# A planned attention and feed-forward kernel: new planner costs, first batch's inputs ahead of the weights, and a sign mask made by GpSimd

## The chip, the cores and the metric

The kernel runs on one core of one Trainium2 chip. Its time is device microseconds from start to end of one execution; the times shown are medians of several runs. The engines are TensorE (PE, matmuls; PEld is its weight load), VectorE (DVE), ScalarE (ACT), GpSimd (POOL) and SyncE (SP, which issues the DMAs here). Each works through its own instructions in the order in which they were written, and waits on semaphores for the others.

## The reference

```
def _attn_ref(q, k, v, p):                       # 8 batches, 8 heads, 576 tokens, head size 64, 32 packed
    def sm_attn(qq, kk, vv):
        s = scale * np.matmul(qq, kk.transpose(0, 1, 3, 2))
        a = np.exp(s - np.max(s, axis=-1, keepdims=True))
        return np.matmul(a / (np.sum(a, axis=-1, keepdims=True) + 1e-09), vv)
    p_packed = sm_attn(p, k, v)
    return sm_attn(q, p_packed, p_packed)

def _moe_ref(x, w_in, w_out, a, b):              # x 4608 x 512, w_in 512 x 2048, w_out 2048 x 512
    h = x @ w_in
    P = a[0] + a[1] * h + a[2] * h**2 + a[3] * h**3
    Q = 1.0 + np.abs(b[0]) * np.abs(h) + np.abs(b[1]) * h**2
    return (P / (Q + 1e-6)) @ w_out
```

The heads of the attention's output, side by side, are x. Both weight matrices arrive as float64, as pairs of 32-bit words.

## The kernel before, in words

The work runs over 8 batches. For each, `attention(bb)` transposes keys and queries, makes packed values `PPT` from the 32 packed queries, and leaves the transposed softmax weights of the second attention in `AH` (and a low part `AL` from batch 1 on). `m_chunk` multiplies PPT by a chunk of `win`, so that a hidden value takes only the 32 packed rows of each head. A *unit* is one batch, one half of the tokens (288) and one of 8 chunks of 256 hidden columns: 128 units in all. `hidden(bb, x, c)` makes the unit's hidden values h on PE, the polynomials P and Q on ACT, DVE and POOL, and the quotient by Ln and Exp on ACT. `acc_block` multiplies the result (`gh`, and its low part `gl`) by the output weights three units later (`LAG = 3`). The first 12 units (`PLAIN`) use float32 matmuls and later ones split operands into two parts (`split`: high part by ACT, low part `gl` by POOL).

The weights are loaded and converted in 16 *words*, each a block of 128 partitions x 1024 float64 (1 MB, in two DMAs): 8 chunks of `w_in` and 8 of `w_out`, sorted by the unit that first uses them (the first five are `w_in`). `load_words(n)` issues loads until n words are ahead of the converted ones. `convert()` (line 429) turns one word into float32 with two ACT instructions, one mask, and two more DVE instructions (a shift with OR, an integer add); all of them take every second 32-bit element of a row. The mask keeps the sign bit of the rescaled high half and is written where the low half was, so it follows the second ACT instruction, and the two other DVE instructions follow it.

`load(bb, what)` issues the DMAs of one input of a batch: keys `k0`, `k1`, values `v0`, `v1`, queries `q0`, `q1` (for batch 0 of 512 KB each) and the small pieces `r`, `p`, `qr`, `rv` for the remaining 64 tokens and the packed queries. `p` comes with a copy on POOL. The loop at line 923 lists, for batch 0, loads by name and, as numbers, how many words are to be loaded by then. `nc.pin()` behind it fixes the order of all this at the front of the queues.

Nothing else is issued in program order. `nc` is a `Planner`: it records all instructions, prices each one (`cost`, `price`, `transfer`), finds the dependences (`edges`) and simulates the five engines (`schedule`), alternately forward in time and backward to get ranks; it keeps the best of `ROUNDS` forward plans by its own reckoning, and `issue` then writes each engine's instructions in the order of their planned starts. A plan's error thus shows as an engine that waits in front of an instruction with ready ones behind it. `WAY` and `PASS` are delays from one engine's result to another's start, `DMA_ISSUE`, `DMA_DELAY` and `DMA_RATE` price a DMA. `idle` (line 992) puts small dummy matmuls with zeros into planned PE gaps of over 180 ns in the first 150 us of the plan, once the first `acc` matmul is out.

Of the kernel before, what the change touches and what calls it, by code (L numbers as in the profile page):

```python
# [13 lines left out]
F32 = mybir.dt.float32  # L14
F32R = mybir.dt.float32r
I32 = mybir.dt.int32
# [3 lines left out]
ALU = mybir.AluOpType  # L20
AX = mybir.AxisListType
PSUM = bass.MemoryType.PSUM

P = 128
# [7 lines left out]
class Planner:  # L32
# [4 lines left out]

    ENGINES = ("tensor", "vector", "scalar", "gpsimd", "sync")

    COST = {"vector": (70, 1.04), "scalar": (93, 0.83), "gpsimd": (215, 2.11), "tensor": (15, 0.417)}  # L40
    TRANSPOSE, F32 = (15, 0.834), (30, 1.667)
    WAY = {("vector", "vector"): 127, ("scalar", "scalar"): 143, ("tensor", "tensor"): 0, ("gpsimd", "gpsimd"): 0}
    WAY.update({(f"sync", x): 0 for x in ENGINES})
    PASS = 200
    ROUNDS = 4
    DMA_ISSUE, DMA_DELAY = 600, 2300

    DMA_RATE = 100.0, 190.0, 370.0

# [26 lines left out]
    def cost(self, engine, name, args, kwargs):  # L76
        if engine == "sync":
            return self.DMA_ISSUE
        fixed, per = self.COST[engine]
        if engine == "tensor":  # L80
            if name == "transpose" or args[1].dtype == F32:
                fixed, per = self.TRANSPOSE if name == "transpose" else self.F32
        aps = [x for x in args if isinstance(x, bass.AP)]
        if engine == "scalar":
            fixed += (aps[-1].space == PSUM) * -42 + ("accum_out" in kwargs) * 186 + ("bias" in kwargs) * 93
        if engine == "vector" and len(aps) > 2 and any(self.columns(x) == 1 for x in aps[1:]):
            fixed += 60
        if engine == "vector" and name == "tensor_scalar":
            per /= 2
        return fixed + per * self.columns(aps[1] if name.startswith("reduce") else aps[0])  # L90
# [13 lines left out]
    def price(self, engine, calls):  # L104
        if engine != "tensor":
            return sum(self.cost(engine, *x) for x in calls)

        parts = {}
        for name, args, kwargs in calls:
            part = args[1].offset // args[1].ap[0][0], args[0].offset // args[0].ap[0][0]  # L110
            parts[part] = parts.get(part, 0) + self.cost(engine, name, args, kwargs)
        return max(parts.values()) + 7 * (len(calls) - 1)

    def edges(self):

# [30 lines left out]
            edges.append(before)  # L146
        return edges

    def schedule(self, before, after, rank, back=None):

        n = len(rank)
        need = [len(x) for x in before]
        at, start, end = [0.0] * n, [0.0] * n, [0.0] * n
        soon = {e: [] for e in self.ENGINES}
        ready = {e: [] for e in self.ENGINES}
        free = dict.fromkeys(self.ENGINES, 0.0)
        for i in range(n):
            if not need[i]:
                heapq.heappush(soon[self.ops[i][0]], (0.0, rank[i], i))
        now = dma = 0.0  # L160
        left = n
        while left:
            for e in self.ENGINES:
                while soon[e] and soon[e][0][0] <= now:
                    heapq.heappush(ready[e], heapq.heappop(soon[e])[1:])
                if free[e] > now or not ready[e]:
                    continue
                _, i = heapq.heappop(ready[e])
                left -= 1
                start[i] = now  # L170
                end[i] = free[e] = now + self.costs[i]
                if e == "sync":
                    dma = max(dma, end[i]) + self.transfers[i]
                    end[i] = dma + self.DMA_DELAY
                for j in after[i]:
                    need[j] -= 1
                    f = self.ops[j][0]
                    way = self.WAY.get((e, f) if back is None else (f, e), self.PASS)
                    at[j] = max(at[j], end[i] + way)
                    if not need[j]:  # L180
                        heapq.heappush(soon[f], (at[j], rank[j], j))
            now = min(
                t
                for e in self.ENGINES
                for t in ([free[e]] if ready[e] else [max(soon[e][0][0], free[e])] if soon[e] else [1e12])
            )
        return start, end

    def order(self):
        n = len(self.ops)  # L190
        self.costs = [self.price(*x) for x in self.ops]
        self.transfers = [self.transfer(calls[0][1]) if engine == "sync" else 0 for engine, calls in self.ops]
        before = self.edges()
        after = [[] for _ in range(n)]
        for i, x in enumerate(before):
            for j in x:
                after[j].append(i)
        rank = list(range(n))
        best = None
        for r in range(self.ROUNDS):  # L200
            start, end = self.schedule(before, after, rank)
            if best is None or max(end) < best[0]:
                best = self.best = max(end), start, end
            s, e = self.schedule(after, before, [-x for x in end], True)
            m = max(end)
            rank = [m - x for x in e]
            rank[: self.pinned] = range(-self.pinned, 0)
        self.end, self.start = best[0], best[1]
        self.deps, self.t0 = dict(enumerate(before)), best[1]
        return sorted(range(n), key=lambda i: (best[1][i], i))  # L210
# [47 lines left out]
def attention_rational_ffn(  # L258
# [42 lines left out]
    nc = Planner(tc.nc)  # L301
# [76 lines left out]
    def load_words(n):  # L378
        while len(words_in) < min(len(words), converted + n):
            r = len(words_in)  # L380
            kind, i, n2 = words[r]
            used = [x for x, _ in words_in]
            free = [x for x, end in room if r < end and x not in used[converted:]]
            free = [x for x in free if x[0] is not w_ring or x[1] not in (2, 3) or started]
            if not free:
                return
            x = min(free, key=lambda x: max((j for j in range(r) if used[j] == x), default=-1))
            raw = x[0].at(x[1], [P, n2 * 512], I64)
            if kind == "in":
                c = i // 2  # L390
                for y in range(2):
                    src = w_in[2 * y * P : (2 * y + 2) * P, c * CF : (c + 1) * CF].rearrange("(x p) f -> p x f", p=P)
                    nc.sync.dma_start(raw[:, 512 * y : 512 * (y + 1)].rearrange("p (x y) -> p x y", x=2), src)
            else:
                for y in range(n2):
                    nc.sync.dma_start(raw[:, 512 * y : 512 * (y + 1)], w_out[(i + y) * P : (i + y + 1) * P, :])
            words_in.append((x, raw))
# [31 lines left out]
    def convert():  # L429
        nonlocal converted  # L430
        if converted == len(words):
            return
        load_words(AHEAD)
        (kind, i, n), raw = words[converted], words_in[converted][1]
        x = 4 if kind == "in" else n
        w = raw.bitcast(I32).rearrange("p (x y two) -> p x y two", x=x, two=2)
        lo, hi = w[:, :, :, 0], w[:, :, :, 1]

        if kind == "in":
            dst = win[:, i // 2]  # L440
            di = dst.bitcast(I32)
        else:
            dst = undivided(i // 2)
            di = dst.bitcast(I32)
        nc.scalar.activation(hi.bitcast(F32), hi.bitcast(F32), AF.Copy, scale=REBIAS)

        nc.scalar.activation(di, lo.bitcast(U32), AF.Copy, scale=2.0**-29)
        nc.vector.tensor_scalar(lo, hi, -0x80000000, None, ALU.bitwise_and)
        nc.vector.scalar_tensor_tensor(hi, hi, 3, lo, ALU.logical_shift_left, ALU.bitwise_or)
        nc.vector.tensor_add(dst.bitcast(I32), hi, di)  # L450
        converted += 1
        load_words(AHEAD)
# [467 lines left out]
        elif i == 1:  # L920
            nc.sync.dma_start(ov, o)

    for what in (2, "r", 3, "p", "k0", "k1", "qr", 4, "rv", "v0", "v1", 5, "q0", "q1"):
        if isinstance(what, int):
            load_words(what)
        else:
            load(0, what)
# [6 lines left out]
    for _ in range(PRE):  # L934
        convert()
# [105 lines left out]
```

## Time and profile before

| | |
|---|---|
| time, median of 3 runs | 787.98 us (786.75 to 788.15) |
| the profiled execution, first to last instruction (span) | 786.0 us |
| median time beyond that span | 1.98 us |
| mean granted TensorE clock | 0.987 |
| PE busy / DVE / ACT / POOL | 745.8 / 693.2 / 657.8 / 453.6 us |
| moved by DMA | 56.03 MB, 71 GB/s in the mean |
| mask on DVE | 16 instructions |

The profile gives the profiled execution's own time as its span; times of runs contain what lies before the first and behind the last instruction as well. "Busy" is the time in which an engine has an instruction under way, and matmuls' ends are modelled, so a busy PE can still hold slack. In a row of the timeline the bracket at the end is the idle time of that engine just before, with what ended it. In a row of a group, the first figures behind the bar are busy time in us and the mean of one instruction in ns. Nearly every row has line 226, the planner's `issue`, so that groups are told apart by tile names: `m` and `w` are buffers that first hold raw words, `win` the converted `w_in`, `nat` natural-order keys, queries and values, `kx` and `small` attention's scratch, `h` and `acc` matmul results.

### The profile page before, as it was taken

How to read it: one execution, taken by the hardware profiler on the slowest of the kernel's cores; microseconds unless marked ns; L12 is line 12 of the kernel's file. 1: busy time of each engine (PE TensorE's matmuls, PEld its weight loads, DVE VectorE, ACT ScalarE, POOL GpSimd, SP SyncE). 2: the span in 40 equal slices, each digit the busy share in tenths (PEclk: the TensorE clock that was granted, in tenths of full speed). 3: DMA queues.
4: the chain of work that ended last, by engine and by line, in shares of the span. 5: the costliest groups of instructions: out<-in, count | busy, mean ns of one | idle time of the engine just before them, and what ended most of it. 6: DMA issues, size and time to landing. Idle time of an engine off the chain costs nothing.

```text
span 786.0 us, 14945 instructions
## 1 busy us (share of the span) xinstructions
PE 745.8 (95%) x5336; PEld 567.5 (72%) x5336; DVE 693.2 (88%) x1295; ACT 657.8 (84%) x1464; POOL 453.6 (58%) x448
## 2 busy tenths in 40 slices
PE   2679999999999999999999999999999999999997
PEld 1345555588778887678778887678787887778886
DVE  4899999998999789998999789998999789988873
ACT  5869978988896998888897898889798788998872
POOL 0012448757585665756686555756587556766663
PEclk9959999999999999999999999999999999999999
DMA  9984353023601155023601136023701132000001
GB/s 297 332 296 143 108 100 49 1 85 46 110 1 55 45 66 90 1 85 46 95 17 55 44 52 104 1 58 62 94 28 54 41 45 46 1 22 7 27 1 41
DMA packets 152027, 56.03 MB, mean 71 GB/s; under 512 B 122256, under 2 KB 141200, under 8 KB 151952
## 3 DMA queue, kind: packets, MB, share of 16 engines
q1 hardware_dynamic: 151952, 55.07, 30.7%
q8 instruction: 42, 0.69, 0.4%
q14 instruction: 33, 0.27, 0.1%
HBM read 45.62 MB, written 9.44 MB: 70 GB/s over the span
## 4 chain that ended last, share of the span: by engine, by line
PE 76%; ACT 10%; DVE 8%; DMA 4%; issue 1%; POOL 0%; SPq 0%; DVEq 0%; ACTq 0%
PE acc L226 38%; PE h L226 24%; PE at L226 14%; DVE Y L226 4%; ACT Y L226 2%; DMA nat<-in_k_dram 2%; DVE w L226 2%; ACT V L226 1%; ACT U L226 1%; ACT sq L226 1%; ACT kx L226 1%; ACT w L226 1%; DMA m<-in_moe_w_in_dram 1%; ACT m L226 1%; DVE small L226 1%
## 5 line engine op out<-in xcount | busy, mean ns | idle before, releaser
L226 POOL TENSOR_TENSOR U<-U,sq 128x576 f32<-128x576 f32 x128 | 184.1, 1438 | 109.1 <-ACT U L226 55.8
L226 PE MATMUL acc<-w,gh 128*128 128x512 f32 x736 | 239.3, 408 | 1.6 <-ACT gh L226 1.4
L226 PE MATMUL h<-AH,m 128*128 128x288 f32 x1024 | 201.1, 320 | 7.9 <-DVE Y L226 5.6
L226 PEld LDWEIGHTS h<-AH,m 128*128 128x128 f32 x1024 | 163.0, 191 | 45.8 <-DVE Y L226 22.6
L226 POOL TENSOR_TENSOR gl<-Y,gh 128x512 fp32r<-128x512 f32 x116 | 150.2, 1295 | 39.0 <-issue 14.3
L226 PEld LDWEIGHTS acc<-w,gh 128*128 128x128 f32 x736 | 131.8, 188 | 45.5 <-issue 11.8
L226 PE MATMUL acc<-w,gl 128*128 128x512 f32 x384 | 147.9, 412 | 0.0
L226 ACT ACTIVATE Y<-h,abS 128x288 f32<-128x288 f32 x256 | 126.3, 511 | 23.2 <-PE h L226 19.7
L226 ACT ACTIVATE sq<-h 128x288 f32<-128x288 f32 x256 | 107.0, 419 | 39.2 <-PE h L226 31.0
L226 DVE TENSOR_TENSOR Y<-Y,h 128x288 f32<-128x288 f32 x256 | 109.1, 444 | 26.3 <-ACT Y L226 9.7
L226 DVE SCALAR_TENSOR_TENSOR Y<-Y,abS,h 128x288 f32<-128x288 f32 x256 | 124.5, 504 | 2.2
L226 DVE SCALAR_TENSOR_TENSOR Y<-Y,abS,V 128x576 f32<-128x576 f32 x128 | 102.8, 803 | 23.6 <-ACT V L226 23.0
L226 ACT ACTIVATE U<-h 128x288 f32<-128x288 f32 x256 | 98.6, 424 | 9.8 <-PE h L226 4.7
L226 ACT ACTIVATE V<-U,one 128x576 f32<-128x576 f32 x128 | 98.4, 769 | 5.6 <-DVE Y L226 3.8
L226 PE MATMUL h<-AL,m 128*128 128x288 f32 x448 | 96.1, 295 | 0.0
L226 DVE SCALAR_TENSOR_TENSOR V<-U,V 128x576 f32<-128x576 f32 x128 | 96.0, 750 | 0.0
L226 PEld LDWEIGHTS acc<-w,gl 128*128 128x128 f32 x384 | 71.9, 188 | 23.9 <-issue 9.6
L226 DVE SCALAR_TENSOR_TENSOR Y<-V,Y 128x576 f32<-128x576 f32 x116 | 86.7, 748 | 1.9
L226 POOL COPY G<-Y 128x64 f32<-128x64 f32 x116 | 27.5, 237 | 102.6 <-DVE Y L226 95.6
L226 ACT ACTIVATE V<-V 128x576 f32<-128x576 f32 x128 | 84.8, 663 | 0.7
L226 PE MATMUL acc<-half,gh 128*128 128x512 f32 x240 | 78.4, 413 | 1.3 <-ACT gh L226 0.9
L226 ACT CAST gh<-Y 128x512 fp32r<-128x512 f32 x116 | 73.4, 632 | 6.0 <-DVE Y L226 5.5
(135 smaller groups left out, 984.1 us busy)
## 6 DMA issues: line engine op xcount, KB each, us to landing
w<-in_moe_w_out_dram SPq DMA_DIRECT2D x16, 512.0 KB, 4.6
out_dram<-half SPq DMA_DIRECT2D x15, 512.0 KB, 3.1
nat<-in_k_dram SPq DMA_DIRECT2D x48, 144.0 KB, 3.9
nat<-in_q_dram SPq DMA_DIRECT2D x48, 144.0 KB, 4.3
nat<-in_v_dram SPq DMA_DIRECT2D x24, 256.0 KB, 3.7
m<-in_moe_w_in_dram SPq DMA_DIRECT2D x8, 512.0 KB, 6.2
w<-in_moe_w_in_dram SPq DMA_DIRECT2D x8, 512.0 KB, 8.2
nat<-in_k_dram SPq DMA_DIRECT2D x4, 512.0 KB, 7.7
```

What stands on the lines that cost most here:

```text
L226: getattr(getattr(self.nc, engine), name)(*args, **kwargs)
```

## The change

The diff has three parts.

1. The planner's prices and rules. GpSimd, TensorE, ScalarE and way costs get other numbers; a matmul in a tile size other than the one before is charged 95 ns (`SWITCH`, `mode`); a GpSimd instruction and certain VectorE instructions exclude each other (`shares`, `port`); engines start at `FIRST`; at most eight DMAs are in flight (`IN_FLIGHT`), with a delay ahead of and behind each transfer; the backward pass adds 150 ns to each way (`SLACK`); eight rounds are tried instead of four.
2. The pinned loads. Before, two words come first, and five words in all stand ahead of the first batch's queries. After, `r`, `p`, `qr` and the keys come first, then one word, `rv` and the values, a second word, the queries, and the third and fourth word; the fifth is left to the plan.
3. The mask. VectorE's AND with the sign bit becomes GpSimd's comparison of the same values, as float32, with zero, times −2^31.

```
-    COST = {"vector": (70, 1.04), "scalar": (93, 0.83), "gpsimd": (215, 2.11), "tensor": (15, 0.417)}
-    TRANSPOSE, F32 = (15, 0.834), (30, 1.667)
-    WAY = {("vector", "vector"): 127, ("scalar", "scalar"): 143, ("tensor", "tensor"): 0, ("gpsimd", "gpsimd"): 0}
-    WAY.update({(f"sync", x): 0 for x in ENGINES})
+    COST = {"vector": (70, 1.04), "scalar": (93, 0.83), "gpsimd": (150, 2.14), "tensor": (15, 0.418)}
+    TRANSPOSE, F32 = (15, 0.734), (30, 1.62)
+    WAY = {
...
+        ("gpsimd", "scalar"): 75,
+        ("gpsimd", "vector"): 75,
+        ("gpsimd", "tensor"): 100,
...
+    WAY.update({("sync", x): 80 for x in ENGINES})
     PASS = 200
-    ROUNDS = 4
-    DMA_ISSUE, DMA_DELAY = 600, 2300
+    FIRST = {"tensor": 700.0, "vector": 800.0, "scalar": 2000.0, "gpsimd": 1400.0, "sync": 700.0}
+    ROUNDS = 8
+    SWITCH = 95
+    SLACK = 150
+    IN_FLIGHT = 8
+    DMA_ISSUE, DMA_START, DMA_END = 420, 1400, 1200
...
+        if engine == "gpsimd" and len(aps) < 3:
+            fixed, per = 135, 0.9
...
+    def shares(self, engine, calls):
+        if engine == "gpsimd":
+            return True
+        if engine != "vector":
+            return False
+        name, args, _ = calls[0]
+        aps = [x for x in args if isinstance(x, bass.AP)]
+        if any(x.space == PSUM for x in aps):
+            return False
+        return name in ("tensor_scalar", "tensor_copy") or (name == "tensor_add" and aps[0].dtype == I32)
...
+                if e == "sync" and not back and len(landed) >= self.IN_FLIGHT and landed[-self.IN_FLIGHT] > now:
+                    free[e] = landed[-self.IN_FLIGHT]
+                    continue
...
+                s = now
+                if e == "tensor" and not back and self.modes[i] != mode:
+                    s += self.SWITCH
+                    mode = self.modes[i]
+                if not back and self.shared[i]:
+                    s = max(s, port["vector" if e == "gpsimd" else "gpsimd"])
+                    port[e] = s + self.costs[i]
...
+                        dma = max(dma, s + self.DMA_START) + self.transfers[i]
+                        end[i] = dma + self.DMA_END
+                        landed.append(end[i])
...
+                    way = self.WAY.get((f, e) if back else (e, f), self.PASS)
+                    way += self.SLACK * (back and way > 0)
...
-        nc.vector.tensor_scalar(lo, hi, -0x80000000, None, ALU.bitwise_and)
+        nc.gpsimd.tensor_scalar(lo, hi.bitcast(F32), 0.0, -2.0**31, ALU.is_lt, ALU.mult)
...
-    for what in (2, "r", 3, "p", "k0", "k1", "qr", 4, "rv", "v0", "v1", 5, "q0", "q1"):
+    for what in ("r", "p", "qr", "k0", "k1", 1, "rv", "v0", "v1", 2, "q0", "q1", 3, 4):
```

More of the change, by code (lines that the diff above doesn't have):

```diff
@@ L38 @@
     ENGINES = ("tensor", "vector", "scalar", "gpsimd", "sync")
-    COST = {"vector": (70, 1.04), "scalar": (93, 0.83), "gpsimd": (215, 2.11), "tensor": (15, 0.417)}
-    TRANSPOSE, F32 = (15, 0.834), (30, 1.667)
-    WAY = {("vector", "vector"): 127, ("scalar", "scalar"): 143, ("tensor", "tensor"): 0, ("gpsimd", "gpsimd"): 0}
-    WAY.update({(f"sync", x): 0 for x in ENGINES})
-    PASS = 200
-    ROUNDS = 4
-    DMA_ISSUE, DMA_DELAY = 600, 2300
+    COST = {"vector": (70, 1.04), "scalar": (93, 0.83), "gpsimd": (150, 2.14), "tensor": (15, 0.418)}
+    TRANSPOSE, F32 = (15, 0.734), (30, 1.62)
+    WAY = {
+        ("scalar", "scalar"): 105,
+        ("scalar", "vector"): 145,
+        ("scalar", "tensor"): 170,
+        ("scalar", "gpsimd"): 225,
+        ("vector", "vector"): 122,
+        ("vector", "scalar"): 115,
+        ("vector", "tensor"): 140,
+        ("vector", "gpsimd"): 150,
+        ("gpsimd", "scalar"): 75,
+        ("gpsimd", "vector"): 75,
+        ("gpsimd", "tensor"): 100,
+        ("tensor", "tensor"): 0,
+        ("gpsimd", "gpsimd"): 0,
+    }
+    WAY.update({("sync", x): 80 for x in ENGINES})
+    PASS = 200
+    FIRST = {"tensor": 700.0, "vector": 800.0, "scalar": 2000.0, "gpsimd": 1400.0, "sync": 700.0}
[4 more added lines that the diff above has]
+    DMA_ISSUE, DMA_START, DMA_END = 420, 1400, 1200
     DMA_RATE = 100.0, 190.0, 370.0
@@ L84, in cost @@
         if engine == "scalar":
-            fixed += (aps[-1].space == PSUM) * -42 + ("accum_out" in kwargs) * 186 + ("bias" in kwargs) * 93
+            fixed += (aps[-1].space == PSUM) * -42 + ("accum_out" in kwargs) * 93 + ("bias" in kwargs) * 93
+            per += 0.1 * any(x.ap[-1][0] == 2 for x in aps[:2])
+        if engine == "gpsimd" and len(aps) < 3:
+            fixed, per = 135, 0.9
         if engine == "vector" and len(aps) > 2 and any(self.columns(x) == 1 for x in aps[1:]):
@@ L111, in price, with mode @@
             parts[part] = parts.get(part, 0) + self.cost(engine, name, args, kwargs)
-        return max(parts.values()) + 7 * (len(calls) - 1)
+        wide = len(calls) > 4 and self.columns(calls[0][1][0]) > 256
+        return max(parts.values()) * (1.15 if wide else 1) + 7 * (len(calls) - 1)
+    def shares(self, engine, calls):
[8 more added lines that the diff above has]
+        return name in ("tensor_scalar", "tensor_copy") or (name == "tensor_add" and aps[0].dtype == I32)
+    def mode(self, engine, calls):
+        name, args, _ = calls[0]
+        if engine != "tensor" or name == "transpose":
+            return None
+        size = args[1].ap[0][1], self.columns(args[1])
+        return None if size == (P, P) else size
     def edges(self):
@@ L147, in edges, with schedule @@
         return edges
-    def schedule(self, before, after, rank, back=None):
+    def schedule(self, before, after, rank, back=False):
         n = len(rank)
@@ L155, in schedule @@
         ready = {e: [] for e in self.ENGINES}
-        free = dict.fromkeys(self.ENGINES, 0.0)
+        free = dict.fromkeys(self.ENGINES, 0.0) if back else dict(self.FIRST)
+        port = {"vector": 0.0, "gpsimd": 0.0}
+        mode, landed, dma = None, [], 0.0
         for i in range(n):
@@ L159, in schedule @@
                 heapq.heappush(soon[self.ops[i][0]], (0.0, rank[i], i))
-        now = dma = 0.0
+        now = 0.0
         left = n
@@ L167, in schedule @@
                     continue
+                if e == "sync" and not back and len(landed) >= self.IN_FLIGHT and landed[-self.IN_FLIGHT] > now:
+                    free[e] = landed[-self.IN_FLIGHT]
+                    continue
                 _, i = heapq.heappop(ready[e])
                 left -= 1
-                start[i] = now
-                end[i] = free[e] = now + self.costs[i]
-                if e == "sync":
-                    dma = max(dma, end[i]) + self.transfers[i]
-                    end[i] = dma + self.DMA_DELAY
+                s = now
[5 more added lines that the diff above has]
+                    port[e] = s + self.costs[i]
+                start[i] = s
+                end[i] = free[e] = s + self.costs[i]
+                if e == "sync":
+                    if back:
+                        dma = max(dma, end[i]) + self.transfers[i]
+                        end[i] = dma + self.DMA_START + self.DMA_END - self.DMA_ISSUE
+                    else:
+                        dma = max(dma, s + self.DMA_START) + self.transfers[i]
+                        end[i] = dma + self.DMA_END
+                        landed.append(end[i])
                 for j in after[i]:
@@ L177, in schedule @@
                     f = self.ops[j][0]
-                    way = self.WAY.get((e, f) if back is None else (f, e), self.PASS)
+                    way = self.WAY.get((f, e) if back else (e, f), self.PASS)
+                    way += self.SLACK * (back and way > 0)
                     at[j] = max(at[j], end[i] + way)
@@ L192, in order @@
         self.transfers = [self.transfer(calls[0][1]) if engine == "sync" else 0 for engine, calls in self.ops]
+        self.shared = [self.shares(*x) for x in self.ops]
+        self.modes = [self.mode(*x) for x in self.ops]
         before = self.edges()
@@ L204, in order @@
             s, e = self.schedule(after, before, [-x for x in end], True)
-            m = max(end)
+            m = max(e)
             rank = [m - x for x in e]
```

## The prediction

> **What bounds the kernel now.** I read the page first: span, busy shares, slices and the shares of the chain.
>
> ```profile
> span 786.0 us, 14945 instructions
> PE 745.8 (95%) x5336; PEld 567.5 (72%) x5336; DVE 693.2 (88%) x1295; ACT 657.8 (84%) x1464; POOL 453.6 (58%) x448
> ...
> PE   2679999999999999999999999999999999999997
> ...
> PEclk9959999999999999999999999999999999999999
> ...
> PE 76%; ACT 10%; DVE 8%; DMA 4%; issue 1%; POOL 0%; SPq 0%; DVEq 0%; ACTq 0%
> ```
>
> TensorE is busy 745.8 of 786.0 us and carries 76% of the chain; only the first three slices (19.65 us each) lack work. So I cut the span into stages: up to 113 us (weights converted, first batch's attention, first units), then stretches of two batches.
>
> ```profile
> 0.00:113.00 113.00, 83.31 (x668) 47.46 (x669) 96.41 (x175) 89.65 (x172) 26.33 (x24) 0.91 0.66 215
> 113.00:283.26 170.26, 170.05 (x1159) 126.28 (x1161) 153.11 (x293) 147.51 (x335) 110.61 (x107) 1.00 0.26 50
> 283.26:461.78 178.52, 176.76 (x1332) 140.33 (x1336) 162.77 (x308) 153.44 (x352) 113.53 (x115) 1.00 0.31 55
> 461.78:640.28 178.50, 176.77 (x1333) 140.34 (x1336) 161.90 (x307) 152.85 (x350) 113.12 (x114) 1.00 0.31 55
> 640.28:786.00 145.72, 138.91 (x861) 113.10 (x860) 119.05 (x215) 114.35 (x258) 90.01 (x91) 1.00 0.11 25
> ```
>
> The columns are start:end, length, busy time of PE, PEld, DVE, ACT and POOL (instructions), granted clock, DMA share, GB/s. Of 40.2 us without a matmul, 113 − 83.31 = 29.7 lie in the first stage, 0.2 + 1.8 + 1.7 in the next three, 6.8 in the last with its closing copy and store. A better order has little to take after 113 us; before it there is much. That stage in pieces:
>
> ```profile
> 0.00:15.00 15.00, 0.00 (x0) 0.00 (x0) 6.12 (x8) 7.16 (x7) 1.31 (x7) 1.00 0.91 292
> 15.00:31.00 16.00, 12.05 (x180) 9.28 (x180) 11.69 (x28) 13.26 (x29) 0.58 (x1) 1.00 1.08 346
> 40.00:54.00 14.00, 8.94 (x41) 5.10 (x40) 12.64 (x19) 9.13 (x17) 2.35 (x2) 0.62 0.81 275
> 54.00:61.00 7.00, 6.32 (x25) 3.02 (x26) 6.56 (x12) 5.76 (x12) 1.42 (x1) 0.50 0.96 366
> 61.00:80.00 19.00, 18.65 (x100) 10.10 (x100) 17.59 (x30) 18.14 (x37) 5.18 (x4) 0.95 0.36 116
> 80.00:100.00 20.00, 19.30 (x129) 10.51 (x131) 19.95 (x37) 18.91 (x42) 7.14 (x5) 1.00 0.30 105
> ```
>
> Up to 31 us the DMA engines are full; from 61 us PE, DVE and ACT are all close to full, and no one of them alone is the bound. The chain of waits, then the timeline, name what is late:
>
> ```profile
> 2.25 7.69 DMA m<-in_moe_w_in_dram
> ...
> 9.95 5.10 DMA nat<-in_k_dram
> ...
> 29.66 9.84 DMA nat<-in_k_dram
> ...
> 40.00 5.30 DMA w<-in_moe_w_in_dram
> ...
> 47.62 2.96 DVE w L226 x3
> ...
> 53.79 4.22 PE h L226 x8
> ```
>
> ```profile
> 4.72 3.60 SPq L226 DMA_DIRECT2D pn<-in_p_dram  x4
> 6.06 1.13 ACT L226 ACTIVATE m<-m 128x1024 f32<-128x1024 f32 x1 [4.04 <-DMA m<-in_moe_w_in_dram]
> 15.19 1.08 PE L226 MATMUL at<-ident,nat 128*128 128x128 f32 x4 [15.19 <-DMA nat<-in_k_dram]
> 28.12 0.42 PEld L226 LDWEIGHTS acc<-ident,w 128*128 128x128 f32 x4 [0.26 <-DMA w<-in_q_dram]
> 39.57 0.90 SPq L226 DMA_DIRECT2D w<-in_moe_w_in_dram  x2
> 43.28 2.29 PE L226 MATMUL h<-AH,m 128*128 128x288 f32 x4 [1.60 <-DVE AH L226]
> 45.39 1.19 ACT L226 ACTIVATE w<-w 128x1024 f32<-128x1024 f32 x1 [4.87 <-DMA w<-in_moe_w_in_dram]
> ```
>
> Keys reach PE at 15.19 us, behind three words; queries at 28.12, behind five. The first matmul of `hidden` comes at 43.28. ACT then stands 4.87 us in front of a word issued only at 39.57, although unit 0's activations are ready behind it; unit 1 starts at 53.79.
>
> **The change, part by part.** *Loads moved.* A word is 128 x 1024 x 8 bytes = 1.05 MB, a 512 KB load 0.52. Ahead of the keys' end stood three words (3.15), r 0.13, p 0.07 and the keys 1.05: 4.4 MB, which is what 292 GB/s brings in 15 us. After, r, p, qr and the keys, 1.38 MB, are nine issues on SP's queue, and no word precedes them. Bounds for the keys' arrival: 6 us (one word, nearly as many bytes, was read at 6.06) and 12 us (p's four issues alone took 3.60; all nine at that pace take 8.1, and the last has still to land). I take 9, nearer to the byte count with some pause for small issues: 6 us earlier. Queries had 8.85 MB up to their end (4.38 in 15 us, the rest at 346 GB/s, gives 27.9; they were used at 28.12). After it is two words and the attention inputs, 5.7 MB: 15 + 1.32/0.346 = 18.8 us, with the late start about 20, so 8 earlier. Values pass one word more than keys and come at about 16, where the chain 6 us earlier needs them at 18 or later (an estimate: the attention chain, 15.19 to 28.12, shifted). So `hidden` starts some 6 us earlier: −6, ends −9 and −3. The words moved back pay: ACT's first work moves from 6.06 to 9, and the conversions fall among the attention's copies. ACT has 89.65 us of work before 113, so this is +3; ends 0 (hidden in its later gaps) and +6.
>
> *Word 6 and the order after the pinned part.* The new plan lets a load start only when one of eight in flight has landed, and counts 1.4 us before and 1.2 us behind the transfer. That is what the 39.57 row violated: the old plan reckoned the word landed long before. I expect ACT no longer to be put in front of it: −4 of the 4.87. Ends −5 and 0, since batch 1's keys (9.84 us in the chain) still share the bandwidth.
>
> *The mask on GpSimd.* Sixteen instructions leave DVE and sixteen join POOL.
>
> ```profile
> L226 DVE TENSOR_SCALAR w<-w 128x1024 int32<-128x1024 int32 x12 | 9.7, 808 | 1.4 <-ACT win L226 1.4
> L226 DVE TENSOR_SCALAR m<-m 128x1024 int32<-128x1024 int32 x4 | 2.8, 698 | 8.4 <-ACT win L226 8.4
> L226 POOL COPY G<-Y 128x64 f32<-128x64 f32 x116 | 27.5, 237 | 102.6 <-DVE Y L226 95.6
> L226 POOL TENSOR_TENSOR gl<-Y,gh 128x512 fp32r<-128x512 f32 x116 | 150.2, 1295 | 39.0 <-issue 14.3 <-ACT gh L226 12.0 <-POOL G L226 6.3
> 40.77 0.29 POOL L226 COPY pn<-pn 128x128 f32<-128x128 f32 x1 [25.19 <-DMA pn<-in_p_dram]
> 104.89 1.26 POOL L226 TENSOR_TENSOR w<-w,w 128x512 fp32r<-128x512 f32 x1
> 105.19 2.05 DVE L226 CUSTOM_DVE_ANT_0 w<-w,w 128x2048 uint16<-128x2048 uint16 x1
> L226 DVE CUSTOM_DVE_ANT_0 win<-m,win 128x2048 uint16<-128x2048 uint16 x4 | 4.9, 1223 | 0.1
> ```
>
> DVE is relieved of 9.7 + 2.8 = 12.5 us. GpSimd's price for 1024 columns isn't shown. Copies of 64 and 128 columns took 0.237 and 0.29 us, 0.83 ns a column: 1.03 us. Two-input adds took 1.295 for 512: 2.6 us. With one input the copies are nearest: 1.1 us, ends 1.0 and 2.6. A word is then 0.4 us (to 1.9) longer on its way, on words that wait anyway. POOL was busy 26.33 of 113 us; 16 x 1.1 = 18 fit. But it slows DVE: the integer add takes 1.22 us alone and 2.05 beside a POOL add, +0.83. With a third of 16 words hit, DVE gives back 4 and gains 8 net. Worth in time: nothing if ACT (18.91 of 20 us) or PE (19.30) bounds 61 to 113, at most 8 if DVE alone does; I take −2.
>
> The Trainium skill (GPSIMD Engine Reference, Performance pitfalls for Q7 kernels) gives about 1.9 cycles an element for reads whose stride stays within 8 bytes, as this one's does; at 1.2 GHz that is an estimate of 1.6 us a mask, and the sum would move by at most 0.5 us a word, hidden but for the first ones. The same page (Key points) says that GpSimd shares its SBUF interfaces with VectorE and contends with two-port modes or two-input instructions; the 2.05 us row agrees.
>
> *The new costs after 113 us.* Mode switches, shared-port delays, ways between engines, eight rounds instead of four: they add no work, only order. PE's gaps in the three middle stretches sum to 3.7 us. I take −1; ends −4 and +17 (rival below). Dummy matmuls follow planned gaps:
>
> ```profile
> L223 PE MATMUL acc<-w,zero 128*64 128x96 f32 x20 | 2.1, 251 | 0.0
> ```
>
> Their number can go to none or double: −2 to +2, taken at 0.
>
> *Clock.* PE ran at 0.62 and 0.50 of its clock from 40 to 61 us; unit 1's eight matmuls took 4.22 us. I keep that, shifted. If PE stays warm, about half of 4.22 is saved; inside the range. The Trainium skill (TensorE: Matmul & The Clock Gate, What's actually happening) puts the halving behind an idle window of about 3.4 us. By that rule a denser start would keep the clock. No row here proves it for or against.
>
> *Sum.* −6 + 3 − 4 − 2 − 1 = −10 on the span of 786.0: 776. The median of the runs shown is 787.98, 1.98 beyond it, for what lies outside the span: 778.
>
> **The rivals.** *A second gain* (the plan also packs the middle): PE's 3.7 us of gaps, 2 us fewer dummies, 2 us of clock and unit 1's full 5 us instead of 4 make some 8 more: 770. Against it: gaps this small follow dependences, not only order.
>
> *ACT stays the bound and keeps its gaps.* From 6.06 to 113 it has 107 − 89.65 = 17.3 us of them. Started at 9, with 4.9 of the gaps gone: 9 + 89.65 + 12.4 = 111, −2: 786, no change that can be told or a hair faster. For it: 18.14 of 19 and 18.91 of 20 busy. Against: its late gaps are waits on PE and DVE, which get work earlier.
>
> *GpSimd's results planned too early.* The new plan prices a 512-column GpSimd add at 150 + 2.14 x 512 = 1246 ns plus 100 to TensorE: 1.35 us. The old one had 1295 + 200 = 1.50, and the row has 1.295 for the add alone. If PE comes to the 116 products with `gl` up to 0.15 us early and stands, that is 17 us, from 113 us to the end: 776 + 17 + 2 = 795. It decides from 10/116 = 0.09 us a unit. For it: every unit has one. Against: the product follows by three units (`LAG`), so there is room, and no PE wait on POOL stands among the larger waits now.
>
> *The mask moved to no effect on DVE*, if shared-port hits eat all 12.5 us (15 hits of 0.83): +2, 780; still faster by the loads.
>
> **How the numbers follow.** This kernel's three times spread by 0.2%, so below 0.2% (1.6 us) nothing can be told. The forecast, counting the mask's rival, whose time is within its own range of 771 to 784: 0.59. Second gain: 0.15. ACT the bound: 0.12, of which 0.08 is within 0.2%. GpSimd too early: 0.14, nearly all of it slower. That makes faster 0.78, same 0.08, slower 0.14. The range of 767 to 788 leaves out the slower case and the far end of the second gain.
>
> **What would show it.** Keys' transposes at about 9 us, queries at 20, first `h` at 37; ACT without a DMA wait of several us between 36 and 50; sixteen POOL instructions of about 1.1 us; DVE masks gone, integer adds slower beside POOL; pairs of batches still at 178 us. Wrong would be: PE waits on POOL's `gl` from unit to unit, masks stuck behind a copy that waits for batch 1's p (25.19 us of idle POOL stood before the 40.77 row), or words landing after attention is done.

## The result, and the profile after

The changed kernel took 796.63 us in the median (793.63 to 797.29), against 787.48 for the kernel before on the same chip: a ratio of 1.0114, with an interval of 1.0092 to 1.0137. It is slower by some 9 us; 778 was forecast.

The page of the changed kernel, the same lines as of the kernel before:

```profile
span 795.5 us, 15034 instructions
PE 749.7 (94%) x5350; PEld 571.7 (72%) x5350; DVE 691.2 (87%) x1279; ACT 656.1 (82%) x1464; POOL 516.3 (65%) x464
...
PE   4576989999999999999999999999999999999997
...
PEclk9767999999999999999999999999999999999999
...
PE 77%; ACT 7%; DVE 4%; POOL 4%; DMA 3%; issue 2%; SPq 2%; POOLq 0%; DVEq 0%; ACTq 0%
```

POOL is busy 62.7 us more (516.3 against 453.6) and now has 4% of the chain, where it had none. DVE lost its 16 masks and yet is only 2 us less busy. PE has work earlier (4 in the first slice, 2 before), and lacks it in the fourth (6, 9 before). The stages (columns as before):

```profile
0.00:15.00 15.00, 6.10 (x64) 5.21 (x68) 0.46 (x3) 5.04 (x8) 0.99 (x7) 1.00 0.71 220
...
31.00:40.00 9.00, 2.84 (x32) 0.81 (x32) 9.00 (x18) 5.51 (x10) 4.65 (x2) 0.52 1.05 385
40.00:54.00 14.00, 10.08 (x53) 5.78 (x53) 13.99 (x25) 11.20 (x19) 12.30 (x4) 0.62 0.47 128
54.00:61.00 7.00, 6.09 (x37) 3.68 (x38) 7.00 (x11) 7.00 (x17) 6.75 (x4) 0.92 0.98 303
61.00:80.00 19.00, 11.08 (x57) 5.46 (x55) 13.23 (x19) 10.98 (x24) 11.79 (x6) 0.73 0.33 117
80.00:100.00 20.00, 19.44 (x136) 10.76 (x129) 19.77 (x30) 19.12 (x37) 19.12 (x7) 1.00 0.49 162
```

Two things stand out. In the first 15 us DVE works 0.46 us instead of 6.12. And POOL is nearly full from 40 to 61 us and from 80 to 100; between, from 61 to 80, PE, DVE, ACT and POOL are each at 11 to 13 of 19 us: they wait for one another in turn. The groups by form and the timeline of the changed kernel name it:

```profile
L288 POOL TENSOR_SCALAR w<-w 128x1024 int32<-128x1024 f32 x12 | 51.1, 4272 | 4.1 <-ACT w L288 3.0 <-ACT win L288 1.1
L288 POOL TENSOR_SCALAR m<-m 128x1024 int32<-128x1024 f32 x4 | 15.2, 3808 | 21.8 <-ACT win L288 17.5 <-DMA w<-in_moe_w_in_dram 4.4
```

```profile
60.21 4.77 POOL L288 TENSOR_SCALAR w<-w 128x1024 int32<-128x1024 f32 x1
...
65.01 2.40 DVE L288 SCALAR_TENSOR_TENSOR w<-w 128x1024 int32<-128x1024 int32 x1 [3.68 <-POOL w L288]
...
69.49 2.08 PE L288 MATMUL acc<-w,gh 128*128 128x512 f32 x2 [7.92 <-DVE w L288]
...
72.03 0.37 ACT L288 COPY small<-at 128x256 f32<-128x256 f32 x1 [6.74 <-PE at L288]
```

A mask takes 3.8 to 4.3 us, 66.3 us in sum, where I took 1.1. DVE stands 3.68 us in front of the OR that needs one, with units' work behind it in its queue, PE 7.92 us in front of the products with that word, and ACT then 6.74 us for PE.

Units serve as milestones. Below, in every kernel's trace, the start in us of VectorE's instruction `V<-U,V`, of which each unit has one, for five of the 128 units, with the span. The other kernels are described further down.

```
                                   unit 0  unit 3  unit 12  unit 96  unit 120   span
before                               56.6    82.4    142.6    611.0     737.4  786.0
after                                57.3    92.8    157.1    622.8     746.4  795.5
mask back on VectorE                 53.9    84.3    145.4    612.3     736.1  785.0
mask on GpSimd, true price           70.3    93.3    155.0    621.6     746.2  795.1
before, mask alone                   66.6    93.1    152.4    621.8     748.4  796.9
mask on GpSimd as times zero         53.8    85.1    149.4    615.4     739.1  788.1
before, new planner alone            58.6    82.1    141.5    608.0     731.5  780.5
before, new loads alone              53.3    83.1    145.1    613.4     740.0  788.6
words between the inputs             55.8    81.1    139.6    605.4     729.7  778.6
no mask at all                       51.2    78.8    135.2    602.1     725.7  774.9
words between, no mask               52.3    77.2    133.1    600.3     723.9  773.0
```

After is 14.5 us late at unit 12, and makes up 5.5 by unit 120: the whole loss is in the front, and the later part is faster.

### The profile page after: what moved, and what is told of

Its sections match the earlier page's. It is cut to its first block, busy times and chain, and to the rows that moved or that the text cites. A ratio compares the mean times of both kernels' runs of the same rounds, so it can differ in the third digit from the quotient of the medians.

```text
span 795.5 us, 15034 instructions
## 1 busy us (share of the span) xinstructions
PE 749.7 (94%) x5350; PEld 571.7 (72%) x5350; DVE 691.2 (87%) x1279; ACT 656.1 (82%) x1464; POOL 516.3 (65%) x464
## 4 chain that ended last, share of the span: by engine, by line
PE 77%; ACT 7%; DVE 4%; POOL 4%; DMA 3%; issue 2%; SPq 2%; POOLq 0%; DVEq 0%; ACTq 0%
PE acc L288 40%; PE h L288 24%; PE at L288 13%; POOL w L288 4%; DVE Y L288 2%; SPq L288 2%; ACT V L288 2%; DMA w<-in_moe_w_in_dram 1%; DMA w<-in_q_dram 1%; ACT Y L288 1%; DVE w L288 1%; ACT sq L288 1%; ACT U L288 1%; DMA AH<-in_q_dram 1%; ACT gh L288 1%
## 5 line engine op out<-in xcount | busy, mean ns | idle before, releaser
L288 PEld LDWEIGHTS acc<-w,gh 128*128 128x128 f32 x736 | 133.7, 188 | 51.2 <-DVE w L288 8.2
L288 ACT ACTIVATE U<-h 128x288 f32<-128x288 f32 x256 | 100.3, 423 | 11.8 <-DVE V L288 9.7
L288 PEld LDWEIGHTS h<-AL,m 128*128 128x128 f32 x448 | 71.8, 188 | 1.0 <-issue 0.9
```

The costliest lines, as they stand in the source:

```text
L288: getattr(getattr(self.nc, engine), name)(*args, **kwargs)
```

## The experiments

Each run's ratio is to the kernel before, run again on the same chip. Theories M, L, D and P are named in the expectations.

**Mask back on VectorE (e1).** The changed kernel with one line undone, planned anew.

```
-        nc.gpsimd.tensor_scalar(lo, hi.bitcast(F32), 0.0, -2.0**31, ALU.is_lt, ALU.mult)
+        nc.vector.tensor_scalar(lo, hi, -0x80000000, None, ALU.bitwise_and)
```

> The changed kernel with the mask back on VectorE, planned anew; planner and loads stay new. Theory M (GpSimd's mask, 3.8 to 4.8 us against the 1.06 planned, holds up DVE and PE up to unit 12): the front's loss of 14.5 us goes, unit 12 comes no later than before (142.6 us) and likely 5 to 9 earlier, the gain of 5 us after it stays: 773 to 782 us. Theory L (the new order of loads and the new front of the plan lose the time, the mask only fills gaps of POOL): the front stays some 8 to 14 us behind, 788 to 796 us.

786.38 us, a ratio to before of 0.9965 (0.9952 to 0.9978). The mask on GpSimd costs the difference to 1.0114, 1.5% or some 12 us. But the rest is worth only 2 to 3 us, and unit 12 is still 2.8 us later than before. The time lies in neither theory's range, between the two: theory M holds for the larger part, and the front has a second loss, which it doesn't explain.

**True price for the mask (e2).** The planner is told that the mask takes 3.8 us.

```
+        if engine == "gpsimd" and name == "tensor_scalar":
+            fixed, per = 150, 3.55
```

> The changed kernel, with the planner told 150 + 3.55 ns a column (3.8 us) for the mask. It separates the mask's length from the plan's ignorance of it. If the ignorance is what costs (engines standing in front of a late mask): most of the 14.5 us comes back, 780 to 787 us. If the length itself costs (16 x 4.1 = 66 us of POOL in the first 118 us, which also hold POOL's adds of the units): 789 to 796 us. Theory L: 792 to 797, since the loads are as before.

797.07 us, 1.0113 (1.0096 to 1.013), as the changed kernel. Knowing the length doesn't help, and the plan only moves the loss forward (unit 0 comes at 70.3). The time is just above what the length and what theory L gave, so this run alone doesn't decide between them; the run before and the next one do.

**Mask alone (e3).** The kernel before with the mask's line of the change and nothing else.

> The kernel before with only the mask moved to GpSimd; old planner (which prices it at 215 + 2.11 x 1024 = 2.38 us) and old loads. Theory M: masks of 3.8 us or more again, slower than before by 4 to 14 us, 791 to 801 us. Theory L: within 3 us of before, 785 to 790 us.

798.51 us, 1.0127 (1.0111 to 1.0144): 10 us by the mask alone, with old loads and old planner. That is theory M without any help from the rest.

**Times zero (e8).** A float times zero keeps its sign, so one multiplication makes the mask.

```
-        nc.gpsimd.tensor_scalar(lo, hi.bitcast(F32), 0.0, -2.0**31, ALU.is_lt, ALU.mult)
+        nc.gpsimd.tensor_scalar(lo.bitcast(F32), hi.bitcast(F32), 0.0, None, ALU.mult)
```

> The changed kernel with the mask on GpSimd as one multiplication of the float value by zero, written as float32 (the sign of the zero is the mask). The planner prices it the same, so every engine has the same order, and only the length of 16 POOL instructions differs. If the two-step comparison with an integer result is what is long, the instruction takes 1.0 to 1.6 us (the copies' 0.83 ns a column): theory M then gives 774 to 784 us, theory L 790 to 796 us. If any GpSimd instruction over 1024 strided columns takes 3.8 us, 794 to 799 us by both.

789.84 us, 1.0019 (1.0006 to 1.0032), outside what theory M gave for it, because the instruction wasn't as short as I had thought:

```profile
L288 POOL TENSOR_SCALAR w<-w 128x1024 f32<-128x1024 f32 x12 | 39.0, 3265 | 5.5 <-ACT w L288 3.9 <-ACT win L288 1.3 <-ACT half L288 0.3
L288 POOL TENSOR_SCALAR m<-m 128x1024 f32<-128x1024 f32 x4 | 12.3, 3063 | 21.3 <-ACT win L288 21.3
```

It is 0.75 to 1.0 us shorter than the mask, and the kernel about 7 us faster than the changed one (1.0019 against 1.0114) with the planner's prices unchanged. Length turns into time at the rate of some 7 us for 15. VectorE is as busy as in the changed kernel (692.3 and 691.2 us), so what came back is waiting and not VectorE's work.

**GpSimd's prices (e6).** Sixteen instructions at the end of the kernel with the mask on VectorE, on a tile that nothing reads any more, in a single run (819.47 us, longer by the added work). `row(n, o)` is n columns side by side from column o, `every(n, o)` every second one. The eight forms, each issued twice:

```
+        nc.gpsimd.tensor_copy(row(1020, 1024), row(1020, 0))
+        nc.gpsimd.tensor_copy(every(1016, 0), every(1016, 0))
+        nc.gpsimd.tensor_scalar(row(1012, 1024), row(1012, 0), 0.0, None, ALU.mult)
+        nc.gpsimd.tensor_scalar(every(1008, 0), every(1008, 0), 0.0, None, ALU.mult)
+        nc.gpsimd.tensor_scalar(row(1004, 1024), row(1004, 0), 0.0, -2.0**31, ALU.is_lt, ALU.mult)
+        nc.gpsimd.tensor_scalar(row(1000, 1024).bitcast(I32), row(1000, 0), 0.0, -2.0**31, ALU.is_lt, ALU.mult)
+        nc.gpsimd.tensor_scalar(every(996, 0).bitcast(I32), every(996, 0), 0.0, -2.0**31, ALU.is_lt, ALU.mult)
+        nc.gpsimd.tensor_scalar(every(252, 0).bitcast(I32), every(252, 0), 0.0, -2.0**31, ALU.is_lt, ALU.mult)
```

> The changed kernel with the mask on VectorE and sixteen added GpSimd instructions at its end, on a tile that is no longer read (8 forms, twice, told apart by their number of columns: 1020 copy in a row; 1016 copy of every second column; 1012 and 1008 times zero, in a row and every second; 1004 the comparison times -2^31 in a row as float32; 1000 the same with int32 result; 996 the mask's form, every second and int32; 252 the same with a quarter of the columns). If the stride makes the mask long: 1012 and 1004 near 1.0 us, 1008 near 3. If the arithmetic does: 1020 and 1016 near 1.0, 1012 and 1008 near 3, 1004 to 996 near 3.8. If the int32 result does: 1004 like 1012, 1000 longer. The time itself is some 30 us longer by the added work.

The groups by form of that run (busy us, mean ns behind the bar):

```profile
L288 POOL TENSOR_SCALAR G<-G 128x996 int32<-128x996 f32 x2 | 7.2, 3616 | 0.2
L288 POOL TENSOR_SCALAR G<-G 128x1004 f32<-128x1004 f32 x2 | 7.1, 3570 | 0.2
L288 POOL TENSOR_SCALAR G<-G 128x1000 int32<-128x1000 f32 x2 | 7.1, 3547 | 0.2
L288 POOL TENSOR_SCALAR G<-G 128x1008 f32<-128x1008 f32 x2 | 5.6, 2814 | 0.2
L288 POOL TENSOR_SCALAR G<-G 128x1012 f32<-128x1012 f32 x2 | 5.5, 2752 | 0.2
L288 POOL COPY G<-G 128x1016 f32<-128x1016 f32 x2 | 2.2, 1076 | 0.1
L288 POOL TENSOR_SCALAR G<-G 128x252 int32<-128x252 f32 x2 | 2.1, 1073 | 0.2
L288 POOL COPY G<-G 128x1020 f32<-128x1020 f32 x2 | 2.1, 1034 | 0.1
```

The arithmetic is what is long: a copy takes 1.03 us, one operation 2.75, two 3.57. Stride (1020 against 1016, 1012 against 1008) changes the time per column by 3 to 4.5%, an integer result (1004 against 1000) by less than 1%. From 252 to 996 columns the mask costs (3616 − 1073)/744 = 3.4 ns a column.

**New planner alone (e4), new loads alone (e5), and words between (e9).** Theory M leaves the second loss. Mask on VectorE in all three; the planner or the loop of loads as the change has it, or a third order:

```
e4:  for what in (2, "r", 3, "p", "k0", "k1", "qr", 4, "rv", "v0", "v1", 5, "q0", "q1"):      # new planner
e5:  for what in ("r", "p", "qr", "k0", "k1", 1, "rv", "v0", "v1", 2, "q0", "q1", 3, 4):      # old planner
e9:  for what in (1, "r", "p", "qr", "k0", "k1", 2, "rv", "v0", "v1", 3, "q0", "q1", 4):      # new planner
```

> The kernel before with the new planner only: old loads, mask on VectorE. Theory D (the front is bound by the work of VectorE, so that what counts is when VectorE gets its first words: at 8.2 us with the old loads, at 15.2 with the new): the front is no later than before and the gain of some 4 us after unit 12, seen in the changed kernel and with the mask back on VectorE, stays: 779 to 785 us. Rival P (the new planner makes the front worse, the loads do not): unit 12 some 3 us late as in the run with the mask on VectorE, 785 to 789 us.

782.82 us, 0.9934 (0.9917 to 0.9951): the planner alone is worth 5 us.

> The kernel before with the new order of loads only: old planner, mask on VectorE. Theory D: the keys arrive at 9 us, but VectorE starts 7 us later and the front ends later than before: 789 to 797 us, as the old planner in addition misjudges the loads. Rival P: the front gains the 6 us of the earlier keys: 779 to 784 us.

791.32 us, 1.0041 (1.0025 to 1.0056): the loads alone *cost* 3 us, though the keys come 6.6 us sooner and unit 0 3.3 us sooner (53.3). By unit 3 that is gone.

> The new planner, mask on VectorE, and loads in the order: a word, r, p, qr, keys, a word, rv, values, a word, queries, a word (the new order has the keys ahead of the first word and a word fewer at each point). Theory D: VectorE gets a word at 8 us and keeps the keys' 3 us of gain: 779 to 785 us, 2 to 6 less than with the new order (786.4). If the start of VectorE does not matter: 785 to 789 us, since the keys come 3 us later.

780.15 us, 0.9895 (0.9878 to 0.9912): faster than both kernels, the fastest one with the whole computation. All three times lie in theory D's ranges. The timeline of VectorE and TensorE in this run, then the first 15 us of three runs (mask back on VectorE, new planner alone, words between; third number behind the length's comma is DVE):

```profile
8.89 0.70 DVE L288 TENSOR_SCALAR m<-m 128x1024 int32<-128x1024 int32 x1 [7.35 <-ACT win L288]
...
10.93 1.09 PE L288 MATMUL at<-ident,nat 128*128 128x128 f32 x4 [10.93 <-DMA nat<-in_k_dram]
```

```profile
0.00:15.00 15.00, 5.98 (x44) 4.96 (x50) 0.25 (x2) 4.92 (x8) 1.00 (x7) 1.00 0.72 222
```

```profile
0.00:15.00 15.00, 0.00 (x0) 0.00 (x0) 5.47 (x8) 6.44 (x6) 0.70 (x6) 1.00 0.88 285
```

```profile
0.00:15.00 15.00, 4.07 (x21) 3.88 (x22) 3.40 (x5) 5.27 (x7) 1.00 (x7) 1.00 0.81 247
```

DVE has 0.25, 5.47 and 3.40 us of work in that time. Its first word comes at 16.77, 8.00 and 8.89 us; the 15.2 in the expectations is its first sizeable instruction of any kind, 15.23 with the mask back on VectorE. One word first gives DVE most of its early work back and still has the keys there 4.3 us sooner than before. From 15 to 100 us DVE is nearly full with either order (79.5 us with the mask back on VectorE, 80.1 with words between, of 85), so it doesn't make up the 3.2 us that it lost at the start.

**No mask at all (e11), and the same with words between (e10).** What would a mask for nothing be worth? VectorE's OR takes zeros in its place, so the weights lose their signs.

```
+        none = zero.bitcast(I32)[:, 0:1].rearrange("p (a b) -> p a b", a=1).broadcast_to([P, x, 1024 // x])
-        nc.vector.scalar_tensor_tensor(hi, hi, 3, lo, ALU.logical_shift_left, ALU.bitwise_or)
+        nc.vector.scalar_tensor_tensor(hi, hi, 3, none, ALU.logical_shift_left, ALU.bitwise_or)
```

> The changed kernel without a mask on any engine: VectorE's OR takes a column of zeros in its place, so the weights lose their signs, and all else is planned as with the mask on VectorE (786.4 us). It is what the change could bring if GpSimd made the mask at no cost. Theory D (VectorE's work, 12.5 us of it masks, sets the end of the front): 776 to 782 us, a gain of 4 to 10. If ACT or PE is the bound there: 784 to 787 us, a gain of the predicted 2 us at most.

776.56 us, 0.9846 (0.9824 to 0.9868): 1.2%, some 9 us faster than with the mask on VectorE, for 12.0 us less VectorE work (680.4 against 692.4). That is what theory D gave: DVE's work sets the end of the front. Each word's way also gets one step of 0.7 to 0.8 us shorter by this, which the run doesn't separate.

> The same with the words between the first batch's inputs (780.2 us with the mask on VectorE); again the weights lose their signs. Theory D: 772 to 777 us. If the earlier start of VectorE has already made PE the bound of the front: 778 to 781 us.

774.8 us, 0.9826 (0.9805 to 0.9848): again 5 us less than with the mask. The two orders of loads now differ by 2 us instead of 6, which agrees with an idle VectorE at the start as what made the difference. Whether the later words held up ACT or PE as well was not tested apart from that. Both times without a mask lie in theory D's ranges.

## Why the prediction was wrong, point by point

The parts add up: planner −5 (e4), loads +2 to +3 (e1 against e4, and e5), mask +10 to +12 (e3, and after against e1) make the +9 measured. My sum had −5, −3 and −2.

- *The mask's price* is the step that failed most. I bounded it by 1.0 and 2.6 us and took 1.1, "with one input the copies are nearest". It was 3.8 to 4.3, beyond both ends, and the mask's term of the sum, −2, measured +10 to +12. The nearest row had to be sought by operation, not by the number of inputs: in the probes a copy takes 1.03 us and one multiplication 2.75. The two-input add in the same list, 2.5 ns a column, was nearer to a multiplication (2.7), and no row in the trace of before showed GpSimd at arithmetic with two operations, so the upper end should have been left open. The rule of the Trainium skill that I weighed there (GPSIMD Engine Reference, Performance pitfalls for Q7 kernels), by which I estimated 1.6 us, was nearer than my 1.1 and still less than half of what ran.
- *What a late mask does.* "On words that wait anyway" was wrong once the mask was four times as long: with 66 us of masks in sum, POOL is nearly full from 40 to 61 us, and DVE, PE and ACT wait in turn. This stood under what would make the prediction wrong only as a mask behind a copy; the copies took 0.29 us and waited 4.1 us in all.
- *The worth of relieving DVE.* I gave it 2 us net, since ACT and PE were close to full as well. A mask for nothing is worth 9 to 10 (e11). Busy shares near 1 on three engines don't say which one sets the end; the removal of work did. Nor did GpSimd leave the 8 us net that I had counted: with the mask alone (e3) VectorE is busy 692.4 us, against 693.2 before, so that nearly all of the 12.5 us came back as slower instructions. That was the condition of the rival *the mask moved to no effect on DVE*; its time of 780 missed because it, too, had a short mask. The largest piece is the OR, here before and with the mask alone:

```profile
L226 DVE SCALAR_TENSOR_TENSOR w<-w 128x1024 int32<-128x1024 int32 x12 | 15.0, 1260 | 0.0
L226 DVE SCALAR_TENSOR_TENSOR w<-w 128x1024 int32<-128x1024 int32 x12 | 19.5, 1626 | 3.5 <-POOL w L226 3.5
```

- *Loads: right in the keys, wrong in the balance.* In the changed kernel keys came at 8.81 us (9 predicted), but the first `h` only at 44.60 (37 predicted, 43.28 before):

```profile
8.81 1.09 PE L288 MATMUL at<-ident,nat 128*128 128x128 f32 x4 [8.81 <-DMA nat<-in_k_dram]
...
44.60 4.04 PE L288 MATMUL h<-AH,m 128*128 128x288 f32 x8
```

  With the mask back on VectorE (e1) it does come at 37.29, and the loss shows only behind it:

```profile
37.29 4.21 PE L288 MATMUL h<-AH,m 128*128 128x288 f32 x8 [6.82 <-DVE root L288]
```

  But I costed the words moved back by ACT alone, +3, and nowhere counted DVE's first 15 us: 6.12 us of work before, 0.25 then, on the engine that sets the end of the front. The term was −6 + 3; it measured +2 to +3. If the keys' part was −6, the words' part was 8 to 9, not 3; no run has the two apart.
- *The planner* was right in its sum, −5, by luck, since it was wrong in its place: I had −4 up to unit 12 and −1 behind. With the planner alone, 1.1 us are gained up to unit 12 and 4.8 more up to unit 120. ACT's DMA wait in the front shrank from 4.87 to 2.70 us there rather than to 0.9; in the changed kernel ACT has none between 36 and 50 us, as predicted, and yet is part of a slower front. Which of the planner's many numbers gained the later part was not tried.
- *The slower rival* named GpSimd's `gl` as the late result. The engine was right, the instruction wrong: no wait of PE for `gl` stands among its larger ones, and the part behind unit 12 got faster.
- *The clock* alone doesn't explain the order of the kernels: words between, the fastest with the whole computation, had a granted clock of 0.53 from 31 to 40 and 0.50 from 40 to 54 us. The prediction says of the clock rule that it quotes that no row proves it for or against. Rows of before speak against it here: from 28 to 61 us PE stood for no longer than 1.88 us at a stretch, well short of that rule's window, and the granted clock was 0.62 and 0.50 from 40 to 61 us all the same. The longest stretch:

```profile
53.79 4.21 PE L226 MATMUL h<-AH,m 128*128 128x288 f32 x8 [1.88 <-DVE Y L226]
```

- A time near my 778 would not have shown the sum to be right: with new loads, new planner and no mask at all the kernel takes 776.6 us, with +2 to +3 by the loads where I had −3, and −9 to −10 by VectorE's relief where I had −2.

## What to carry to other kernels

Price an instruction that an engine has not run yet by a row with the same *operation*, and if there is none, leave the upper end open: one probe on the chip is cheaper than a re-plan around a wrong price. When work moves to an idle engine, put the length on the path of the data, not only on the engine's share of busy time. And when inputs are reordered, count for each nearly full engine when its first work arrives; an engine that sets the end of a stage must not start later for the sake of another.

## What the runs showed of the hardware that was not expected

GpSimd's copy of 1020 float columns took 1.03 us, one multiplication by a constant 2.75, a comparison and a multiplication 3.57; stride two and integer results were nearly free. The mask also got longer when it began beside a VectorE conversion. Of the changed kernel's 16 masks, the six that began while VectorE had an OR or an integer add of a word under way took 4.38 to 4.82 us, the other ten 3.75 to 3.94; the probe's rate gives 3.7 for 1024 columns. In the other direction even the smallest VectorE instructions got longer beside a GpSimd one. In the changed kernel the same instruction takes 0.16 us ahead of the first mask, and 1.06 us just behind that mask's start at 16.41 us:

```profile
15.93 0.16 DVE L288 TENSOR_SCALAR small<-small 128x2 f32<-128x2 f32 x1
...
16.45 1.06 DVE L288 TENSOR_SCALAR small<-small 128x2 f32<-128x2 f32 x1
```
